# A recurrence, a gated softmax and a ReLU layer on one core: the hand-over into the last stage in a new order

## The chip, the cores and the metric

The kernel runs on one core of a Trainium2 chip. The engines work side by side, each through its own list of instructions in order, and wait for each other by semaphores: PE (TensorE, matrix products), DVE (VectorE), ACT (ScalarE), POOL (GpSimd) and SP (here only a queue of DMA transfers). The metric is the device time of one execution in microseconds.

## The reference

Three layers follow each other. The first is a recurrence over 768 time steps for 4 batches and 8 heads of width 48; the second a layer with a softmax that multiplies its own input and a normalisation; the third a leaky ReLU layer.

```python
def _attn_ref(r, k, v, w, u):
    ...
    for t in range(S):
        cur = np.einsum('bhd,bhe->bhde', u[None] * kt, vt)
        y[:, :, t] = np.einsum('bhd,bhde->bhe', rt, state + cur)
        state = wt[:, :, :, None] * state + np.einsum('bhd,bhe->bhde', kt, vt)

def _moe_ref(x, w_in, w_out, g_ln):          # x: 3072 x 384, d_ff 1024
    h = x @ w_in
    e = np.exp(h - np.max(h, axis=-1, keepdims=True))
    solu = h * e / (np.sum(e, axis=-1, keepdims=True) + 1e-09)
    mu = np.mean(solu, axis=-1, keepdims=True)
    var = np.mean((solu - mu) ** 2, axis=-1, keepdims=True)
    return ((solu - mu) / np.sqrt(var + 1e-06) * g_ln) @ w_out

def _moe2_ref(x, w_in, w_out):               # d_ff 2048
    h = x @ w_in
    return np.maximum(0.01 * h, h) @ w_out
```

## The kernel before

The weights are 64-bit numbers. Their bits are decoded on the chip into 32-bit ones (`decode_exp`, `decode_val`: L58 and L66 to L72 on DVE, L60 on ACT), and each is split into a rounded part and a rest (`hi`, `lo`). A product of two split matrices takes three passes (`passes`).

**Units.** The 3072 tokens are cut into 24 units of 128 (0 to 23), which go through one loop, each in several turns of it: `prep*` and `att_*` make the recurrence of a unit by blocks of time, `x_t` turns the result, `mm1` multiplies by the first layer's input weights into the PSUM tile PH (18 matmuls), `soft_max`, `soft_z`, `soft_c` and `soft_q` make maximum, exponential, product, centring and sum of squares, `z_t` turns the result through PZ, and `z_hi`, `z_lo` split it. A unit's softmax thus runs a turn after its recurrence. Three units make a group of 384 tokens (0 to 7); `mm2(g, m, part)` multiplies a third m of the output for group g, in two halves of 12 matmuls, into the PSUM tile PO or PK, which `mm2_out` copies (L544 on ACT) and writes to memory (`o1_dram`).

**Last stage.** `load_x2`, `split_x2` fetch and split blocks of 512 tokens of that (0 to 7, 768 KB each). Its unit of work is a step (g, c): block g, column chunk c of 16. `mm3` is 9 matmuls into one of two PSUM tiles `h`; ACT and DVE make the leaky ReLU `t` (L701, L702), ACT rounds it (`gh`, L703), `gw_sub` makes the rest `gw`; two steps later `mm4` adds 9 matmuls to the block's output `acc`. The first 32 steps alternate between blocks 0 and 1, c by c. A finished output is scaled on DVE into one of two buffers `ot` and written out. The last layer's weights are decoded in 32 pieces (16 `w2i`, 16 `w2o`) by `dec_step`, some pieces in the hand-over, and one in each of the first steps of the last stage: `load_w2` fetches a piece, `dec_a` starts it, `dec_b` finishes it, `split_hi` and the function that it returns split it.

**Order.** The code runs under a manual schedule: each engine's order is that of the code. The hand-over is what lies between the last unit's `x_t` and the first `mm3`.

Of the kernel before, what the change touches and what calls it, by code (L numbers as in the profile page):

```python
# [19 lines left out]
TOK = B * S  # L20
# [219 lines left out]
def body(tc, trw, nat, w1p, u_p, r, k, v, w, u, w1i, w1o, gln, w2i, w2o, out):  # L240
# [6 lines left out]
    with ExitStack() as ctx:  # L247
# [116 lines left out]
        def prep_bonus(i):  # L364
            a = nats[i]
            pool.tensor_tensor(out=a[:, 1], in0=a[:, 1], in1=a[:, 2], op=ALU.mult)
            pool.tensor_tensor(out=a[:, 1], in0=a[:, 1], in1=ub, op=ALU.mult)

        def prep_diag(i):
            dg = ap2.tile([128, H, 1], F32, name="dg")  # L370
            dve.tensor_reduce(out=dg, in_=nats[i][:, 1], axis=AX.X, op=ALU.add)
            dgs[i] = dg

        def prep_vd(i):
            d = ap2.tile([128, H, D], F32, name="vd")
            vds[i] = d
            pool.tensor_tensor(out=d, in0=nats[i][:, 0], in1=dgs.pop(i).to_broadcast([128, H, D]), op=ALU.mult)
# [24 lines left out]
        def att_u(i):  # L402
            ks, a = kT.pop(i), nats[i]
            for q in range(4):
                for x in range(2):
                    m = 48 if x else 64
                    for c in range(2):
                        pe.matmul(out=PA[64 * x:64 * x + m, c, 256 + 48 * q:304 + 48 * q],  # L408
                                  lhsT=ks[64 * c:64 * c + 64, 112 * q + 64 * x:112 * q + 64 * x + m],
                                  rhs=a[64 * c:64 * c + 64, 0, 4 * x + q], start=True, stop=True)  # L410
# [13 lines left out]
        def att_next(i):  # L424
# [10 lines left out]
        def att_y(i):  # L435
            lt, s, a = L.pop(i), ss[i % 2], nats.pop(i)
# [10 lines left out]
            for q in range(4):  # L447
                for x, (p, e) in enumerate(rows):
                    h = 4 * x + q
                    hs = slice(48 * h, 48 * h + 48)  # L450
                    for c, y in enumerate((y0, y1)):
                        pe.matmul(out=y[64 * c:64 * c + 64, hs], lhsT=s[64 * c:64 * c + 64, x, q],  # L452
                                  rhs=a[64 * c:64 * c + 64, 0, h], start=(h == 0), stop=False, skip_group_check=True)
# [117 lines left out]
        def w1_a():  # L571
# [6 lines left out]
            else:  # L578
                t = mb.tile([128, 512], I32, name="dt")[:, 0:q.shape[1]]
# [41 lines left out]
        pools = [we]  # L621
        w2o_at = []

        def load_w2():
# [3 lines left out]
            t = pools[-1].tile([128, DM, 2], I32, name="w2s", bufs=2 if len(pools) == 1 else 4)  # L628
# [8 lines left out]
        def dec_a():  # L637
# [3 lines left out]
            t = pools[-1].tile([128, DM], I32, name="w2t", bufs=2 if len(pools) == 1 else 4)  # L641
# [3 lines left out]
        def dec_b():  # L645
# [4 lines left out]
            if len(pools) > 1:  # L650
                load_w2()
# [10 lines left out]
        def split_hi():  # L662
            if not ws or (ws[0][0] == "o" and not w2o_at):
                return None
# [6 lines left out]
            else:  # L671
                hi, lo = w2o_at[0][:, c], w2o_at[1][:, c]
# [3 lines left out]
        def load_x2(g):  # L676
            t = xp.tile([128, KC, 512], F32, name="x2")
# [315 lines left out]
```

## Time and profile before

| | |
|---|---|
| median of 3 runs | 823.58 us (823.12 to 824.87) |
| the profiled execution | 822.63 us, span 820.9 us |
| busy: PE, DVE, ACT, POOL | 755.3 (92%), 552.2 (67%), 355.0 (43%), 185.3 (23%) us |
| unit loop up to unit 23's `x_t` | up to about 364 us of the span |
| hand-over | 364 to 406 us |
| last stage | 406 to 813 us, then the last outputs |

The span is the time from the first instruction to the last in the profiler's record; the execution's own time is a little longer. Shares of busy time are means over stages in which different engines set the pace.

### The profile page before, as it was taken

Reading aid. Unit: us, or ns where it says so; the run is one execution under the profiler, and the core shown is the slowest. Engines: PE = TensorE matmul, PEld = TensorE weight load, DVE = VectorE, ACT = ScalarE, POOL = GpSimd, SP = SyncE. Lnnn points to the kernel's source line nnn. Section 1 sums busy time; section 2 is a strip of 40 time slices with the busy share of each in tenths; the row PEclk is TensorE's granted clock in tenths of the full one; section 3 lists DMA queues with packets and bytes.
Section 4 is the critical chain, followed back from the end, with each engine's and each line's share of the span. In section 5 each row is a group of like instructions: output and inputs, shape, how many; then the busy total and the mean of one; then the engine's idle time right before and its main releaser. Section 6 shows DMA issues by size and latency. Waiting matters only on the chain.

```text
span 820.9 us, 14859 instructions
## 1 busy us (share of the span) xinstructions
PE 755.3 (92%) x6197; PEld 623.6 (76%) x6197; DVE 552.2 (67%) x853; ACT 355.0 (43%) x648; POOL 185.3 (23%) x194
## 2 busy tenths in 40 slices
PE   2677889999999999997788999999999999999996
PEld 1344678888888888887666887888888888888884
DVE  6899898888888888868799997243334334334332
ACT  3445455554645555545444554222322322322221
POOL 2211263544545453500211231000100100100000
PEclk9985999999999999999899999999999999999999
DMA  9710334333333445023633430012002001001001
GB/s 297 270 53 15 122 86 125 108 112 108 112 111 109 125 130 149 13 62 106 229 113 92 164 113 0 1 39 77 1 1 77 1 1 39 0 1 40 0 1 42
DMA packets 27805, 66.60 MB, mean 81 GB/s; under 512 B 3804, under 2 KB 13172, under 8 KB 27604
## 3 DMA queue, kind: packets, MB, share of 16 engines
q1 hardware_dynamic: 27300, 64.02, 24.9%
q10 hardware_dynamic: 432, 1.57, 0.6%
q8 instruction: 50, 0.82, 0.4%
q14 instruction: 23, 0.19, 0.1%
HBM read 56.13 MB, written 9.45 MB: 80 GB/s over the span
## 4 chain that ended last, share of the span: by engine, by line
PE 74%; DVE 17%; DMA 3%; issue 2%; ACT 2%; SPq 0%; POOL 0%; DVEq 0%; ACTq 0%
PE acc L716 20%; PE h L695 19%; PE PH L490 11%; PE PO L539 11%; PE PZ L516 3%; DVE w2s L70 3%; PE PA L452 2%; DMA tr<-in_trw_dram 2%; PE PA L408 2%; DVE w2s L68 2%; PE PA L388 2%; DVE w2t L66 2%; DVE t L702 1%; PE PA L461 1%; DVE w2t L72 1%
## 5 line engine op out<-in xcount | busy, mean ns | idle before, releaser
L702 DVE TENSOR_TENSOR t<-t,h 128x512 f32<-128x512 f32 x96 | 65.8, 686 | 133.9 <-ACT t L701 133.9
L701 ACT ACTIVATE t<-h 128x512 f32<-128x512 f32 x96 | 57.3, 597 | 152.4 <-PE h L695 152.4
L695 PE MATMUL h<-x2h,w2ih 128*128 128x512 f32 x288 | 112.2, 390 | 4.4 <-DVE t L702 4.4
L716 PE MATMUL acc<-gw,w2oh 128*128 128x512 f32 x288 | 113.5, 394 | 1.0 <-DVE gw L708 0.8
L716 PE MATMUL acc<-gh,w2ol 128*128 128x512 f32 x288 | 114.0, 396 | 0.0
L695 PE MATMUL h<-x2h,w2il 128*128 128x512 f32 x288 | 113.9, 395 | 0.0
L695 PE MATMUL h<-x2l,w2ih 128*128 128x512 f32 x288 | 113.6, 395 | 0.0
L716 PE MATMUL acc<-gh,w2oh 128*128 128x512 f32 x288 | 112.6, 391 | 0.0
L703 ACT CAST gh<-t 128x512 fp32r<-128x512 f32 x96 | 59.9, 624 | 104.8 <-DVE t L702 104.8
L708 DVE TENSOR_TENSOR gw<-t,gh 128x512 fp32r<-128x512 f32 x83 | 59.3, 714 | 48.9 <-ACT gh L703 46.2
L695 PEld LDWEIGHTS h<-x2h,w2ih 128*128 128x128 f32 x288 | 54.1, 188 | 17.5 <-DVE t L702 5.3
L716 PEld LDWEIGHTS acc<-gw,w2oh 128*128 128x128 f32 x288 | 54.1, 188 | 15.2 <-DVE gw L708 2.5
L695 PEld LDWEIGHTS h<-x2l,w2ih 128*128 128x128 f32 x288 | 54.0, 188 | 13.4
L716 PEld LDWEIGHTS acc<-gh,w2oh 128*128 128x128 f32 x288 | 54.1, 188 | 12.5
L716 PEld LDWEIGHTS acc<-gh,w2ol 128*128 128x128 f32 x288 | 54.1, 188 | 11.6
L695 PEld LDWEIGHTS h<-x2h,w2il 128*128 128x128 f32 x288 | 54.0, 188 | 11.5
L539 PE MATMUL PO<-zh,w1oh 128*128 128x384 f32 x168 | 61.3, 365 | 0.0
L496 ACT ACTIVATE ebuf<-PH,nmax 128x1024 f32<-128x1024 f32 x24 | 26.8, 1117 | 76.3 <-DVE nmax L495 76.3
L490 PE MATMUL PH<-w1ih,xh 128*128 128x512 f32 x144 | 59.1, 411 | 0.6 <-ACT xh L478 0.6
L490 PE MATMUL PH<-w1ih,xl 128*128 128x512 f32 x144 | 57.1, 396 | 0.0
L539 PE MATMUL PO<-zl,w1oh 128*128 128x384 f32 x168 | 57.0, 339 | 0.0
L490 PE MATMUL PH<-w1il,xh 128*128 128x512 f32 x144 | 57.0, 395 | 0.0
(155 smaller groups left out, 1497.3 us busy)
## 6 DMA issues: line engine op xcount, KB each, us to landing
tr<-in_trw_dram SPq DMA_DIRECT2D x23, 675.9 KB, 4.7
nat<-in_nat_dram SPq DMA_DIRECT2D x24, 576.0 KB, 4.1
w2s<-in_moe_w_in_dram SPq DMA_DIRECT2D x48, 128.0 KB, 2.7
w2s<-in_moe_w_out_dram SPq DMA_DIRECT2D x16, 384.0 KB, 3.1
o_dram<-o SPq DMA_DIRECT2D x24, 192.0 KB, 1.9
x<-o_dram SPq DMA_DIRECT2D x6, 768.0 KB, 5.6
out_dram<-ot SPq DMA_DIRECT2D x18, 256.0 KB, 2.1
zh<-in_w1p_dram ACTq DMA_DIRECT2D x3, 512.0 KB, 7.7
```

Source lines behind the costliest of these rows:

```text
L66: dve.scalar_tensor_tensor(out=t, in0=hw, scalar=-2147483648, in1=t, op0=ALU.bitwise_and, op1=ALU.bitwise_or)
L70: dve.scalar_tensor_tensor(out=f(lw), in0=lw.bitcast(U32), scalar=2.0 ** -32, in1=hw, op0=ALU.mult, op1=ALU.add)
L490: pe.matmul(out=PH[:, half], lhsT=a[:, kc], rhs=c[:, kc, 512 * half:512 * half + 512], start=(n == 0), stop=(n == 8))
L496: act.activation(out=ebuf, in_=flat(PH), func=AF.Exp, bias=nmax[:, i:i + 1], accum_out=s_all[:, i:i + 1])
L516: pe.transpose(PZ[c // 4][:, 128 * (c % 4):128 * (c % 4) + 128], zbuf[:, 128 * c:128 * c + 128], ident)
L539: pe.matmul(out=o2[m], lhsT=a[:, c, 128 * m:128 * m + 128], rhs=d[:, c], start=(c == 0 and q == 0), stop=(c == K1 - 1 and q == 2))
L695: pe.matmul(out=h2, lhsT=a[:, kc, 128 * o:128 * o + 128], rhs=d[:, kc], start=(q == 0), stop=(q == 8))
L701: act.activation(out=t, in_=h2, func=AF.Copy, scale=0.01)
L702: dve.tensor_tensor(out=t, in0=t, in1=h2, op=ALU.max)
L703: act.copy(out=gh, in_=t)
L708: (pool if g == 1 and c < 13 else dve).tensor_tensor(out=gw, in0=t, in1=f(gh), op=ALU.subtract)
L716: pe.matmul(out=acc[g][o], lhsT=a[:, c, 128 * o:128 * o + 128], rhs=d, start=(c == 0 and q == 0), stop=(c == K2 - 1 and q == 2))
```

## The change

**The hand-over** is taken out of the loop and written as a list. Unit 23's maximum follows its product, with one decoding step ahead of it in place of two; the products of group 6 stand between unit 23's `mm1` and its `z_t`.

**The last stage's inputs** are loaded straight into the tile of the rest and split in place (`x2_hi`, `x2_lo`), in three pairs of tiles with homes of their own (`xhl2`). Block 0 is loaded before unit 23's product. The first weights (`w2o` chunks 0 to 7) and the first two steps' tiles have homes that are free before the last stage begins.

**The weights**: four pieces are loaded in the unit loop rather than two, the list `wl` alternates `w2i` and `w2o` three chunks apart, two decoding steps stand in the turn of unit 22, five in the hand-over and one in each step of the last stage but steps 3, 7 and 11. `gw_sub` is always on DVE. **The end**: three buffers `ot`, and the last two chunks' products by output thirds 0, 1 and then 2. **The unit's inputs**: v is loaded apart from r and k, whose tile has two buffers in place of three.

```diff
         def load_nat(i, eng):
-            t = ap2.tile([128, 3, H, D], F32, name="nat", bufs=3)
-            nats[i] = t
-            eng.dma_start(out=t, in_=nat[i])
+            t = ap2.tile([128, H, D], F32, name="natv", bufs=3)
+            q = ap2.tile([128, 2, H, D], F32, name="natq")
+            nats[i] = (t, q)
+            eng.dma_start(out=q, in_=nat[i, :, 1:3])
+            eng.dma_start(out=t, in_=nat[i, :, 0])
...
-        wl = [("i", c) for c in range(9)] + [("o", 0), ("o", 1)]
-        for c in range(2, K2):
-            wl += ([("i", c + 7)] if c + 7 < K2 else []) + [("o", c)]
+        wl = [("i", c) for c in range(3)]
+        for c in range(K2):
+            wl += [("o", c)] + [("i", c + 3)] * (c + 3 < K2)
...
         def dec_step():
-            lo = split_hi()
+            ready = len(wa) > 0
             if len(wa) + len(ws) < 3:
                 dec_a()
-            dec_b()
+            lo = split_hi()
+            if ready:
+                dec_b()
             if lo:
                 lo()
...
+            x2[g] = xhl2[g % 3]
+            sp.dma_start(out=f(x2[g][1]), in_=o1_dram[:, :, 512 * g:512 * g + 512])
+
+        def x2_hi(g):
+            xh, xl = x2[g]
+            act.copy(out=xh, in_=f(xl))
+
+        def x2_lo(g, eng):
+            xh, xl = x2[g]
+            eng.tensor_tensor(out=xl, in0=f(xl), in1=f(xh), op=ALU.subtract)
...
-            (pool if g == 1 and c < 13 else dve).tensor_tensor(out=gw, in0=t, in1=f(gh), op=ALU.subtract)
+            dve.tensor_tensor(out=gw, in0=t, in1=f(gh), op=ALU.subtract)
...
-                    ot = lp.tile([128, 512], F32, name="ot", bufs=2)
+                    ot = lp.tile([128, 512], F32, name="ot", bufs=3)
...
-                if i in (18, 19):
+                if 15 <= i < 19:
                     load_w2()
...
+            xhl2.append([rp.tile([128, KC, 512], F32R, name=f"x2{y}0") for y in "hl"])
+            load_x2(0)
+            i = NU - 1
+            x_hi(i)
+            x_lo(i)
+            soft_c(i - 1)
+            soft_q(i - 1)
+            dec_step()
+            mm1(i, 0)
+            mm1(i, 1)
+            soft_max(i)
+            z_t(i - 1)
+            soft_z(i)
+            z_hi(i - 1, 0)
+            z_hi(i - 1, 1)
+            mm2(6, 1, 0)
+            mm2(6, 1, 1)
+            soft_c(i)
+            z_lo(i - 1, 0)
+            z_lo(i - 1, 1)
+            mm2_out(6, 1)
+            dec_step()
+            mm2(6, 2, 0)
+            z_t(i)
+            z_hi(i, 0)
+            z_hi(i, 1)
+            mm2(6, 2, 1)
+            z_lo(i, 0)
+            z_lo(i, 1)
+            soft_q(i)
+            dve.tensor_reduce(out=anyf, in_=flags, axis=AX.X, op=ALU.max)
+            pe.matmul(out=PA[0:1, 0, 0:1], lhsT=anyf, rhs=ones, start=True, stop=True)
+            mm2_out(6, 2)
+            x2_hi(0)
+            es_mb.close()
+            xp = es2.enter_context(tc.tile_pool(name="xp", bufs=1, side="right", reuse_waits="tile"))
+            for cg in range(2):
+                w2o_at.append([xp.tile([128, 4, DM], F32R, name=f"w2o{y}{cg}") for y in "hl"])
+            xhl2.append([xp.tile([128, KC, 512], F32R, name=f"x2{y}1") for y in "hl"])
+            load_x2(1)
+            mm2(7, 0, 0)
+            dec_step()
+            dve.tensor_scalar(out=flag, in0=PA[0:1, 0, 0:1], scalar1=0.0, scalar2=None, op0=ALU.is_gt)
+            x2_lo(0, dve)
+            mm2(7, 0, 1)
+            mm2_out(7, 0)
+            x2_hi(1)
+            mm2(7, 1, 0)
+            dec_step()
+            mm2(7, 1, 1)
+            x2_lo(1, dve)
+            mm2_out(7, 1)
+            mm2(7, 2, 0)
+            dec_step()
+            dve.memset(csc, -0.5)
+            inv_std(nc, csc, s_all, q_all, csc)
+            mm2(7, 2, 1)
+            mm2_out(7, 2)
             es_p.close()
...
+                mm3(g, c)
+                if n % 4 != 3 or n > 12:
                     dec_step()
-                    gw_sub(g, c)
...
+                if n == 8:
+                    scales()
+                if n == 4:
+                    load_x2(2)
+                if c == 0 and 2 <= g and g + 1 < N2:
+                    load_x2(g + 1)
+                if (c == 8 and 2 <= g or c == 14 and g == 1) and g + 1 < N2:
+                    x2_hi(g + 1)
+                    x2_lo(g + 1, pool)
+                if 2 <= n < len(order) - 1:
                     mm4(*order[n - 2])
+            g = N2 - 1
+            mm4(g, K2 - 3)
+            for c, os in ((2, (0, 1)), (1, (0, 1)), (2, (2,)), (1, (2,))):
+                mm4(g, K2 - c, os)
```

On DVE, after unit 23's input has been split (`xl`, the row L482, L484 in the changed kernel), the kernel before has, from the rest of the first decoded piece on (L58 to L72 decode a piece, L674 or L677 is its rest):

```order
L674 TENSOR_TENSOR w2il_109<-w2t,w2ih_108 128x3x128
L58 TENSOR_SCALAR w2t<-w2s 128x384
L66 SCALAR_TENSOR_TENSOR w2t<-w2s,w2t 128x384
L68 TENSOR_SCALAR w2s<-w2s 128x384
L70 SCALAR_TENSOR_TENSOR w2s<-w2s 128x384
L72 SCALAR_TENSOR_TENSOR w2t<-w2s,w2t 128x384
L674 TENSOR_TENSOR w2il_109<-w2t,w2ih_108 128x3x128
L529 TENSOR_TENSOR zl<-PZ_97,zh 128x4x128
L529 TENSOR_TENSOR zl<-PZ_98,zh 128x4x128
L495 TENSOR_REDUCE nmax<-PH 128x1
L500 SCALAR_TENSOR_TENSOR zbuf,z_all<-PH,ebuf 128x1024
```

In the changed kernel this stands there from `xl` on:

```order
L58 TENSOR_SCALAR w2t<-w2s 128x384
L66 SCALAR_TENSOR_TENSOR w2t<-w2s,w2t 128x384
L68 TENSOR_SCALAR w2s<-w2s 128x384
L70 SCALAR_TENSOR_TENSOR w2s<-w2s 128x384
L72 SCALAR_TENSOR_TENSOR w2t<-w2s,w2t 128x384
L677 TENSOR_TENSOR w2il_109<-w2t,w2ih_108 128x3x128
L497 TENSOR_REDUCE nmax<-PH 128x1
L502 SCALAR_TENSOR_TENSOR zbuf,z_all<-PH,ebuf 128x1024
L531 TENSOR_TENSOR zl<-PZ_97,zh 128x4x128
L531 TENSOR_TENSOR zl<-PZ_98,zh 128x4x128
L58 TENSOR_SCALAR w2t<-w2s 128x384
```

One decoding step instead of two, and none of unit 22's rests `zl`, now stand ahead of the maximum `nmax`.

On ACT, from the rounding `zh` of unit 23 on (L509 squares, L544 copies a product out of PSUM, L684 rounds an input block of the last stage), before:

```order
L509 ACTIVATE ebuf,q_all<-zbuf 128x1024
L544 COPY o_4441<-PO 128x384
L673 CAST w2ih_4269<-w2t 128x3x128
L60 ACTIVATE w2t<-w2t,ebias 128x384
L684 CAST x2h<-x_4450 128x1536
L673 CAST w2ih_4269<-w2t 128x3x128
L60 ACTIVATE w2t<-w2t,ebias 128x384
L684 CAST x2h<-x_4452 128x1536
L544 COPY o_4518<-PK 128x384
L673 CAST w2ih_4269<-w2t 128x3x128
```

and in the changed kernel:

```order
L511 ACTIVATE ebuf,q_all<-zbuf 128x1024
L546 COPY o_4467<-PO 128x384
L685 CAST x2h_4333<-x2l_4334 128x1536
L60 ACTIVATE w2t<-w2t,ebias 128x384
L676 CAST w2ih_108<-w2t 128x3x128
L546 COPY o_4519<-PK 128x384
L685 CAST x2h_4479<-x2l_4480 128x1536
L60 ACTIVATE w2t<-w2t,ebias 128x384
```

The second block's rounding has moved behind the copy of PK; both had stood ahead of it.

On DVE in the last stage, from the ReLU `t` of a step of block 1 to the next ReLU, before (POOL had that block's `gw`):

```order
L702 TENSOR_TENSOR t<-t,h_4663 128x512
L58 TENSOR_SCALAR w2t<-w2s 128x384
L66 SCALAR_TENSOR_TENSOR w2t<-w2s,w2t 128x384
L68 TENSOR_SCALAR w2s<-w2s 128x384
L70 SCALAR_TENSOR_TENSOR w2s<-w2s 128x384
L72 SCALAR_TENSOR_TENSOR w2t<-w2s,w2t 128x384
L674 TENSOR_TENSOR w2ol<-w2t,w2oh 128x384
L702 TENSOR_TENSOR t<-t,h_4693 128x512
```

and in the changed kernel:

```order
L706 TENSOR_TENSOR t<-t,h_4645 128x512
L58 TENSOR_SCALAR w2t<-w2s 128x384
L66 SCALAR_TENSOR_TENSOR w2t<-w2s,w2t 128x384
L68 TENSOR_SCALAR w2s<-w2s 128x384
L70 SCALAR_TENSOR_TENSOR w2s<-w2s 128x384
L72 SCALAR_TENSOR_TENSOR w2t<-w2s,w2t 128x384
L677 TENSOR_TENSOR w2il_4328<-w2t,w2ih_4327 128x3x128
L712 TENSOR_TENSOR gw<-t,gh 128x512
L706 TENSOR_TENSOR t<-t,h_4684 128x512
```

The rest `gw` of block 1 has come to DVE, behind the decoding.

## Rows read from the trace of the kernel before

**Rows 1.** Page, part 2: granted TensorE clock in 40 slices of 20.5 us, tenths.
```profile
PEclk9985999999999999999899999999999999999999
```

**Rows 2.** Chain that ended last, middle of the last stage (start us, us, what).
```profile
528.39 2.08 PE acc L716 x9
```

**Rows 3.** Waits of PE, 406 us to the end (total us, times, longest).
```profile
PE h L695 <- DVE t L702: 4.4, 2, 2.4
PE acc L716 <- DVE gw L708: 0.8, 1, 0.8
PE h L726 <- DVE t L702: 0.7, 1, 0.7
```

**Rows 4.** Timeline of PE across the handover (start us, us, engine, line, operation).
```profile
364.59 0.50 PE L490 MATMUL PH<-w1ih,xh 128*128 128x512 f32 x1 [0.62 <-ACT xh L478]
...
368.93 1.04 PE L516 MATMUL PZ<-ident,zbuf 128*128 128x128 f32 x8
...
381.19 1.93 PE L516 MATMUL PZ<-ident,zbuf 128*128 128x128 f32 x8 [4.61 <-ACT zbuf L506]
...
385.81 0.34 PE L539 MATMUL PK<-zh,w1oh 128*128 128x384 f32 x1
...
389.98 0.34 PE L539 MATMUL PO<-zh,w1oh 128*128 128x384 f32 x1
...
398.97 0.69 PE L539 MATMUL PK<-zh,w1oh 128*128 128x384 f32 x1 [4.67 <-ACT o L544]
...
406.09 0.40 PE L695 MATMUL h<-x2h,w2ih 128*128 128x512 f32 x1
```

**Rows 5.** Timeline of DVE after unit 23's first product.
```profile
368.54 0.36 DVE L58 TENSOR_SCALAR w2t<-w2s 128x384 int32<-128x384 int32 x1 [3.41 <-DMA w2s<-in_moe_w_in_dram]
...
375.32 1.22 DVE L495 TENSOR_REDUCE nmax<-PH 128x1 f32<-128x1024 f32 x1
```

**Rows 6.** Timeline of ACT in the handover.
```profile
379.99 1.15 ACT L506 ACTIVATE zbuf<-zbuf,nm_all 128x1024 f32<-128x1024 f32 x1 [1.78 <-POOL nm_all L502]
...
392.99 1.48 ACT L684 CAST x2h<-x 128x1536 fp32r<-128x1536 f32 x1 [5.56 <-DMA x<-o_dram]
```

**Rows 7.** Page, part 6: DMA issues (count, KB each, median us to landing).
```profile
nat<-in_nat_dram SPq DMA_DIRECT2D x24, 576.0 KB, 4.1
...
x<-o_dram SPq DMA_DIRECT2D x6, 768.0 KB, 5.6
```

**Rows 8.** Timeline of DVE over two steps of the last stage.
```profile
429.01 0.68 DVE L702 TENSOR_TENSOR t<-t,h 128x512 f32<-128x512 f32 x1
...
432.39 0.69 DVE L708 TENSOR_TENSOR gw<-t,gh 128x512 fp32r<-128x512 f32 x1
...
433.00 0.68 DVE L702 TENSOR_TENSOR t<-t,h 128x512 f32<-128x512 f32 x1
...
434.45 1.48 DVE L68 TENSOR_SCALAR w2s<-w2s 128x384 int32<-128x384 int32 x1
...
437.51 0.68 DVE L702 TENSOR_TENSOR t<-t,h 128x512 f32<-128x512 f32 x1
```

**Rows 9.** Timeline of POOL in the same two steps.
```profile
434.42 1.29 POOL L708 TENSOR_TENSOR gw<-t,gh 128x512 fp32r<-128x512 f32 x1 [7.20 <-ACT gh L703]
```

**Rows 10.** Timeline of the end: the last product on PE, the last output on DVE.
```profile
812.87 0.39 PE L716 MATMUL acc<-gh,w2ol 128*128 128x512 f32 x1
...
814.81 0.69 DVE L721 TENSOR_TENSOR ot<-acc,cb 128x512 f32<-128x512 f32 x1 [1.50 <-DMA out_dram<-ot]
```

**Rows 11.** Timelines of POOL and DVE in the unit loop.
```profile
331.26 1.47 POOL L366 TENSOR_TENSOR nat<-nat 128x384 f32<-128x384 f32 x1
...
344.47 1.47 POOL L366 TENSOR_TENSOR nat<-nat 128x384 f32<-128x384 f32 x1
...
350.50 0.55 DVE L371 TENSOR_REDUCE dg<-nat 128x8 f32<-128x384 f32 x1
```

**Rows 12.** Timeline of DVE at the start of the program.
```profile
19.82 1.24 DVE L323 TENSOR_TENSOR_SCAN suf<-tr,sel 112x520 f32<-112x520 f32 x1 [0.26 <-DMA tr<-in_trw_dram]
```

More of the change, by code (lines that the diff above doesn't have):

```diff
@@ L627, in load_w2 @@
             s, c = wl.pop(0)
-            t = pools[-1].tile([128, DM, 2], I32, name="w2s", bufs=2 if len(pools) == 1 else 4)
+            t = we.tile([128, DM, 2], I32, name="w2s", bufs=4)
             if s == "i":
@@ L662, in split_hi @@
         def split_hi():
-            if not ws or (ws[0][0] == "o" and not w2o_at):
+            if not ws or (ws[0][0] == "o" and ws[0][1] >= 4 * len(w2o_at)):
                 return None
@@ L671, in split_hi @@
             else:
-                hi, lo = w2o_at[0][:, c], w2o_at[1][:, c]
+                hi, lo = [x[:, c % 4] for x in w2o_at[c // 4]]
             act.copy(out=hi, in_=t)
@@ L860, in body @@
                         load_tr(n + 3, sp)
-                if mo and i < NU - 1:
+                else:
+                    dec_step()
+                if mo:
                     mm1(i, 0)
@@ L877, in body @@
                 w1_step(i)
-                if att:
-                    att_x(n)
-                if has2 and i < NU:
-                    if i == NU - 1:
-                        mm2(g, m, 0)
+                att_x(n)
+                if has2:
                     mm2(g, m, 1)
                     mm2_out(g, m)
-                if att:
-                    x_t(n)
+                x_t(n)
                 if mo:
                     soft_z(i)
-                if i == NU - 1:
-                    pe.matmul(out=PA[0:1, 0, 0:1], lhsT=anyf, rhs=ones, start=True, stop=True)
-                    dve.tensor_scalar(out=flag, in0=PA[0:1, 0, 0:1], scalar1=0.0, scalar2=None, op0=ALU.is_gt)
@@ L905, in body @@
-                if i > NU:
-                    dec_step()
-            es_ma.close()
+            es_a.close()
+            rp = es2.enter_context(tc.tile_pool(name="rp", bufs=1, side="right", reuse_waits="tile"))
+            for cg in range(1, 4):
+                w2i_h.append(rp.tile([128, KC, 512], F32R, name=f"w2ih{cg}"))
+                w2i_l.append(rp.tile([128, KC, 512], F32R, name=f"w2il{cg}"))
+            xhl2.append([rp.tile([128, KC, 512], F32R, name=f"x2{y}0") for y in "hl"])
+            load_x2(0)
@@ L911, in body @@
             ps_o = es2.enter_context(tc.tile_pool(name="ps_o", bufs=2, space=PSUM, reuse_waits="tile"))
[L912 to L915 removed]
             order = [(g, c) for c in range(K2) for g in range(2)]
             order += [(g, c) for g in range(2, N2) for c in range(K2)]
[L918 to L930 removed]
+            for n in range(len(order)):
+                if n == 2:
+                    es_ma.close()
+                    lp = es2.enter_context(tc.tile_pool(name="lp", bufs=1, reuse_waits="tile"))
+                    for cg in range(2, 4):
+                        w2o_at.append([lp.tile([128, 4, DM], F32R, name=f"w2o{y}{cg}") for y in "hl"])
+                    xhl2.append([lp.tile([128, KC, 512], F32R, name=f"x2{y}2") for y in "hl"])
+                    cb = lp.tile([128, TOK], F32, name="cb")
+                    lp_at.append(lp)
+                g, c = order[n]
+                mm3(g, c)
+                if n % 4 != 3 or n > 12:
+                    dec_step()
+                gw_sub(g, c)
+                if n == 8:
[8 more added lines that the diff above has]
+                if 2 <= n < len(order) - 1:
```

160 lines of the change are left out of this document (46 added, 114 removed).

## The prediction

> **What bounds the kernel now.** I went from the end backwards. In the chain that ended last, the middle of the last stage is nothing but PE: 9 matmuls take 2.08 us and the next 9 follow at once [rows 2], so a step of 18 takes 4.16 us and the 96 steps at least 399.4 us. The stage starts at 406.09 [rows 4], and its last matmul starts at 812.87 [rows 10] and is passed some 0.23 later (2.08 by 9): 407.0 us. So 7.6 us of the stage are not PE's work. The view of PE's waits names 5.9 of them: 4.4 and 0.7 for the ReLU on DVE, 0.8 for a rest `gw` on DVE [rows 3].
>
> PE's timeline then shows the hand-over. Its first matmul stands at 364.59. At 381.19 PE has waited 4.61 us for unit 23's centred product, at 398.97 another 4.67 us for ACT to free a PSUM tile [rows 4]. The granted clock falls there: the slice from 390 to 410 us has an 8 in a long row of nines [rows 1], so that part of it ran at the lower of the two levels (1.2 and 2.4 GHz). Its price stands in PE's timeline. At full clock 24 products take 4.17 us (385.81 to 389.98); after the second wait the same 24 take 7.12 (398.97 to 406.09), 2.95 more. After the first wait 8 transposes and 12 products take 4.62 us (381.19 to 385.81), against 1.04 for such transposes at 368.93 and half of 4.17: 1.5 more [rows 4].
>
> **Why PE waits.** The first wait is DVE's order. Unit 23's product is done at 368.93, when the next work on PE starts [rows 4], but the maximum starts on DVE at 375.32 [rows 5]. Up to 368.54 DVE waits 3.41 us for a piece of weights, and two pieces and unit 22's rests stand in its list ahead of the maximum [rows 5]. The second wait is ACT's order: it stands 5.56 us at the rounding of an input block whose transfer has not landed, up to 392.99 [rows 6], and the copy that frees PE's tile is behind that.
>
> **The hand-over after the change.** PE's instructions are the same ones, so I take away what its timeline shows as waiting and as lower clock. Will the waits be gone?
> *Unit 23's softmax.* From the start of the maximum (375.32) to the start of the transposes (381.19) the chain takes 5.87 us [rows 4, 5], with POOL's step in it, for which ACT waited 1.78 [rows 6]. One decoding step is still ahead of the maximum. Such a step is 2.7 us: a whole round of DVE in the last stage takes 3.99 (429.01 to 433.00), of which `gw` is 0.61 (432.39 to 433.00) and the ReLU 0.68 [rows 8]. It lies beside the product (364.59 to 368.93, 4.34 us), and its piece is one of four loaded units earlier, so the 3.41 us wait for a piece has no ground. The maximum then starts at about 369.1 and the transposes can start at 375.0. Meanwhile PE has unit 22's transposes and 36 products of group 6, 1.0 plus 6.3 us, up to about 376.2. The wait is covered with about 1 us to spare; without that cover each us of delay would cost one, and after some us the clock too.
> *The input blocks.* Block 0 is asked for during unit 23's product, some 10 us before ACT rounds it, and a transfer takes 5.6 us [rows 7]. Block 1 is asked for behind the output of (6, 2), whose last product ends at 379.3 (376.2, transposes, 12 products) and is copied by 380; so it lands at 386 and is rounded (1.48, as in [rows 6]) at 387.5. Behind that rounding on ACT stand one decoding step's two instructions and the copy out of (7, 1); the copy that frees PK for (7, 2) is ahead of it. DVE must then end the decoding step, of whose 2.7 us under 2 can still be open, and make block 1's rest (taken like the rounding), by about 391; PE reads it with the stage's second `mm3`, at about 394.5. That is 3 us to spare.
> So both waits (4.61 + 4.67) and both stretches at the lower clock (1.5 + 2.95) go: **13.7 us**, and the last stage starts at 392.4. The 0.62 us before unit 23's product stays. The bounds are 0 (both waits come back elsewhere) and 14.3.
>
> **The last stage.** While weights are decoded, DVE sets the pace: two steps take 8.50 us there (429.01 to 437.51) and 8.32 on PE. The step of block 0 takes 3.99, that of block 1 takes 4.51, although POOL makes its `gw` [rows 8]. Without `gw` it should take 3.38, so 1.13 are lost in it. The row shows where: an L68 of 1.48 us, which ends when POOL's subtraction does (434.42 plus 1.29) or just behind [rows 8, 9]. With `gw` on DVE both steps take 3.99, 7.98 for two, under PE's 8.32. The 13 subtractions cost DVE 13 x 0.61 = 7.9 us and spare it 13 x 1.13 = 14.7.
> The Trainium skill, "SBUF — State Buffer", section "SBUF: two separate sides", says that DVE and GpSimd share a pair of ports under an exclusive lock, held for the whole instruction. The trace agrees (1.48 beside 1.29). The rule speaks against what POOL keeps, block 2's rest with three times the columns: by an estimate of 3 x 1.29 = 3.9 us it would hold DVE once, and the sum would be 806.0 if PE felt all of it. I set it at nothing: it stands at step 29, the last with decoding, and from there DVE has 4.16 less 0.68 and 0.61, 2.9 us a step, without work.
> More decoding falls into the stage than before: 6 of 32 pieces are finished when it starts, 11 before, since the hand-over is shorter. The chunk c of `w2o` is split in step 2c+1 from c = 6 on and read in the next one's `mm4`. From the end of `mm3` it takes ACT's part of the ReLU (taken like DVE's, with 0.2 to start, 0.9), DVE's 0.68 and 2.7, 4.3 in all; PE reads the rest of the chunk 4.16 plus two matmuls later, 4.6. That is tight, 0.3 us, but holds. Three steps without decoding (3, 7, 11) let DVE catch up ahead of the transposes of step 8, where PE waits now (L726). I take the 5.9 listed and 1.0 of the 1.7 unlisted as gone, and 0.6 as new waits in the first steps, where DVE still ends the hand-over's last piece: **6.3 us**. Bounds: 0 (DVE still paces) and 7.6.
>
> **The end.** The last output waits 1.50 us on DVE for the transfer that frees one of two buffers [rows 10]. A third buffer removes it: the last product is over by 813.3, when DVE can start. **1.5 us**; bounds 1.0 and 1.6. The new order of the last products only makes the first two outputs earlier.
>
> **Costed at nothing.** The split of v from r and k: as many bytes, 24 more transfers on SP. The load for unit n+2 now waits for the sum `dg` of unit n (two buffers), and all later transfers on SP are behind it. `dg` runs at 350.50; POOL multiplies the next unit's r and k about 7 us after `dg` (344.47 against 350.50 less 13.21) and that of unit n+2 one period later, 331.26 to 344.47 being 13.21 [rows 11]. So 20.4 us lie between, and the transfer takes 4.1 [rows 7]. At the start of the program DVE is nearly always busy and waited only 0.26 us for unit 1's inputs at 19.82 [rows 12]; the transfers ahead of them are the same bytes, so I give it 0, and 1 us either way to the range. Decoding in unit 22 and the split in place are the same instructions as before.
>
> **Sum.** 13.7 + 6.3 + 1.5 = 21.5 us off the profiled 822.63: 801.1. The median of the runs is 0.95 above that execution: 802.1.
>
> **The rivals.**
> *A, the sum:* 802.1, its own range 799.5 to 804.5.
> *B, DVE goes on pacing the first third of the last stage.* For it: DVE's 7.98 is only 4% under PE's 8.32, the margin for `w2o` is 0.3 us, and five more pieces must be decoded there. Against it: the long L68 is explained by POOL. It gives back 6.3: 808.4.
> *C, the hand-over closes in part.* The margin of 1 us for the transposes, or the 3 us for block 1, is used up by a late POOL step or transfer. A wait of 2 us with 1.5 for the clock gives 805.6.
> *D, the waits come back whole elsewhere in the hand-over,* so that the list does not do what it says: 802.1 + 13.7 = 815.8. Against it: nothing ahead of the chains is left that waits.
> *E, slower.* The split loads hold SP, and each unit's inputs come late. From unit 2 to 23 each unit must last 1.0 us longer (21.5 by 22) to eat the gain; at 1.2 us the time is 828.5. It decides when the transfer needs more than 16 us longer than the 4.1 that it takes, for which nothing speaks.
> The Trainium skill, "DMA: Bandwidth & Descriptors", section "Anatomy of one DMA — SWDGE (gpsimd) path", gives every transfer a fixed 2.0 us. By that rule an estimate for 24 more transfers with none hidden is 48 us; the trace's 20.4 us of lead say that all of it is hidden.
>
> **How the numbers follow.** A 0.62, B 0.15, C 0.15, D 0.05, E 0.03. The range is 799 to 808.5: below, all upper bounds (14.3 + 7.6 + 1.6 = 23.5, so 800.1) and 1 us from the start; above, B. It leaves out D, E and a part of B, some 0.15. A change of 0.2% (1.6 us) is about what a measurement of this kernel can tell from none. Faster 0.96, the same 0.01, slower 0.03.
>
> **What would show it.** PE at unit 23's product still near 364.6, which settles the start, E and the split loads. No wait at unit 23's transposes near 376, none at a product into PK, and the granted clock at one through the hand-over; the first `mm3` near 392.4. In the last stage waits of PE under 1.5 us in total, no L68 of 1.48, two DVE steps in 8.32 with idle time in them. The third `ot` without a wait for a transfer. I would be wrong if PE's waits moved to the first `mm3` of block 1 (a late block 1), to `acc` behind a rest of `w2o` (B), or if units lasted longer than 13.21.

## The result

| | before | changed |
|---|---|---|
| median of the runs | 823.46 us (4 runs) | 802.91 us (4 runs, 799.17 to 803.66) |
| ratio of the medians, 95% interval | | 0.9738 [0.9706, 0.9771] |
| the profiled execution | 822.63 us, span 820.9 us | 803.08 us, span 801.0 us |

The forecast of 802.1 us was right in size; its last term was not right in cause, and its middle term hid a cost that I had not seen. That the sum comes so close is in part luck: its errors have both signs, and the start of the hand-over alone scatters by more (below). The difference of the two spans is 19.9 us. PE's timeline divides it: unit 23's product starts 0.9 us later, from there to the first `mm3` 14.26 us are gone, from there to the end of the last product 4.96, and behind it 1.6.

**The hand-over.** The timeline of PE in the changed kernel (start us, us, engine, line, operation, then the wait):
```profile
365.49 0.50 PE L492 MATMUL PH<-w1ih,xh 128*128 128x512 f32 x1 [0.62 <-ACT xh L480]
...
376.97 1.03 PE L518 MATMUL PZ<-ident,zbuf 128*128 128x128 f32 x8
...
388.57 0.34 PE L541 MATMUL PK<-zh,w1oh 128*128 128x384 f32 x1
...
392.73 0.40 PE L698 MATMUL h<-x2h,w2ih 128*128 128x512 f32 x1
```
Against [rows 4] the bracket at unit 23's transposes and the one at the product into PK are gone; the 0.62 ahead of the product stays. From 365.49 to 392.73 are 27.24 us, where it was 41.50. The table of busy time by stretch shows the clock with it (stretch, its us, PE busy, granted clock, DMA share, GB/s), first before, then changed:
```profile
364.60:406.10 41.50, 32.22 (x157) 0.88 0.54 174
```
```profile
365.50:392.70 27.20, 27.20 (x156) 1.00 0.47 153
```
PE worked 32.22 us in the one and 27.20 in the other on the same products, so 9.3 us were the waits', and most of the other 5.0 the lower clock's. The timeline of DVE shows why the first wait went:
```profile
370.05 1.22 DVE L497 TENSOR_REDUCE nmax<-PH 128x1 f32<-128x1024 f32 x1 [0.88 <-PE PH L492]
```
The maximum [rows 5] now waits for the product itself, not for a piece of weights. And the timeline of ACT, for both:
```profile
374.14 1.16 ACT L508 ACTIVATE zbuf<-zbuf,nm_all 128x1024 f32<-128x1024 f32 x1 [0.61 <-POOL nm_all L504]
...
384.61 0.48 ACT L546 COPY o<-PK 128x384 f32<-128x384 f32 x1 [1.70 <-PE PK L541]
...
387.64 1.48 ACT L685 CAST x2h<-x2l 128x1536 fp32r<-128x1536 f32 x1 [2.55 <-DMA x2l<-o_dram]
```
The centred product is ready at 375.30, 1.7 us before PE's transposes. ACT still waits for an input block, as in [rows 6], but the copy that frees PK stands ahead of that wait and is done at 385.1, long before PE comes to PK at 388.57.

**The last stage.** The waits of PE over 360 to 801 us (total us, times, longest), which answer to [rows 3], are all of them these two:
```profile
PE PH L492 <- ACT xh L480: 0.6, 1, 0.6
PE acc L722 <- DVE gw L712: 0.5, 1, 0.5
```
Two steps on DVE, as in [rows 8]:
```profile
425.49 0.69 DVE L706 TENSOR_TENSOR t<-t,h 128x512 f32<-128x512 f32 x1 [1.86 <-ACT t L705]
...
429.78 0.69 DVE L706 TENSOR_TENSOR t<-t,h 128x512 f32<-128x512 f32 x1 [0.21 <-ACT t L705]
...
431.24 0.36 DVE L68 TENSOR_SCALAR w2s<-w2s 128x384 int32<-128x384 int32 x1
...
433.98 0.69 DVE L706 TENSOR_TENSOR t<-t,h 128x512 f32<-128x512 f32 x1
```
No L68 of 1.48 us is left, and no other decoding instruction of DVE in the stage that takes over 0.6. But the chain that ended last shows what I had not expected (start us, us, what). In chunks 0 to 7:
```profile
435.42 2.08 PE h L698 x9
437.50 2.11 PE acc L722 x9
```
in chunks 8 to 15:
```profile
493.90 2.07 PE h L698 x9
495.97 2.09 PE acc L722 x9
```
and in block 2:
```profile
546.10 2.10 PE acc L722 x9
548.20 2.10 PE h L698 x9
```
Nine matmuls took 2.08 in both products before [rows 2]. Now `mm4` takes 2.11 to 2.12 with chunks 0 to 7 of `w2o`, and both products take 2.10 in blocks 2 and 5, whose input lies in the third pair of `x2` tiles (from chunk 8 on, `mm4` takes 2.09 there). Nothing waits in these places: the matmuls themselves follow at 232 to 235 ns instead of 231. On PE's timeline steps 10 to 89 (counted from 0, as in the prediction) take together 1.7 us more than 4.16 each; the stage's 402.05 us are 1.35 above the forecast.

**The end.** The last product on PE, then the outputs on DVE, which answer to [rows 10]:
```profile
794.55 0.39 PE L722 MATMUL acc<-gh,w2ol 128*128 128x512 f32 x1
```
```profile
792.94 1.37 DVE L726 TENSOR_TENSOR ot<-acc,cb 128x512 f32<-128x512 f32 x2 [1.37 <-PE acc L722]
794.98 0.69 DVE L726 TENSOR_TENSOR ot<-acc,cb 128x512 f32<-128x512 f32 x1 [0.67 <-PE acc L722]
```

### The profile page after: what moved, and what is told of

It reads as the page before. It is cut to its first block, busy times and chain, and to the rows that moved or that the text cites. A ratio compares the mean times of both kernels' runs of the same rounds, so it can differ in the third digit from the quotient of the medians.

```text
span 801.0 us, 14910 instructions
## 1 busy us (share of the span) xinstructions
PE 751.9 (94%) x6197; PEld 620.8 (77%) x6197; DVE 547.5 (68%) x866; ACT 354.9 (44%) x648; POOL 167.0 (21%) x181
## 4 chain that ended last, share of the span: by engine, by line
PE 87%; DVE 6%; DMA 2%; ACT 2%; issue 1%; POOL 0%; SPq 0%; DVEq 0%; ACTq 0%; POOLq 0%
PE acc L722 25%; PE h L698 24%; PE PH L492 11%; PE PO L541 11%; PE PZ L518 3%; PE PA L454 2%; DMA tr<-in_trw_dram 2%; PE PA L410 2%; PE PA L390 2%; PE PA L463 1%; PE PO L608 1%; PE PK L386 1%; PE PZ L475 1%; PE PA L444 1%; PE PK L541 1%
## 5 line engine op out<-in xcount | busy, mean ns | idle before, releaser
L712 DVE TENSOR_TENSOR gw<-t,gh 128x512 fp32r<-128x512 f32 x96 | 69.1, 719 | 47.4 <-ACT gh L707 44.6
L689 POOL TENSOR_TENSOR x2l<-x2l,x2h 128x1536 fp32r<-128x1536 f32 x4 | 14.1, 3515 | 285.4 <-ACT x2h L685 285.4
```

Source lines behind the costliest of these rows:

```text
L712: dve.tensor_tensor(out=gw, in0=t, in1=f(gh), op=ALU.subtract)
```

## The experiments

In each, "hand-over" is the time on PE's timeline from the first matmul of unit 23's product to the first `mm3` (27.24 us in the changed kernel), and "stage" that from there to 0.23 us behind the start of the last matmul (402.05). They come from one profiled execution of each kernel; the start of unit 23's product, which no experiment touches, lies anywhere from 361.87 to 367.36 us in them, so whole times carry a scatter of some us. With the changed order these lengths don't: where no edit bears on it, the hand-over is 27.23 to 27.25 each time. With the old order it is 41.50, 40.35 and 40.15 in three executions (before, 2, 7), as its two waits come out at 4.0 to 4.7.

| kernel | median us | ratio to before, 95% interval | hand-over | stage |
|---|---|---|---|---|
| changed | 802.91 | 0.9738 [0.9706, 0.9771] | 27.24 | 402.05 |
| 1: 32 bytes, last stage | 800.17 | 0.9704 [0.9681, 0.9727] | 27.24 | 399.07 |
| 2: before, `w2o` moved by 32 bytes | 826.56 | 1.0030 [1.0011, 1.0049] | 40.35 | 411.88 |
| 3: `gw` on POOL | 806.18 | 0.9781 [0.9757, 0.9805] | 27.23 | 407.94 |
| 4: late maximum | 804.59 | 0.9756 [0.9729, 0.9783] | 28.79 | 401.99 |
| 5: two `ot` | 802.46 | 0.9740 [0.9706, 0.9775] | 27.25 | 402.78 |
| 6: 416 bytes, last stage | 794.01 | 0.9635 [0.9608, 0.9661] | 27.23 | 392.95 |
| 7: before, 416 bytes | 818.15 | 0.9932 [0.9908, 0.9956] | 40.15 | 403.54 |
| 8: block 1 first on ACT | 804.15 | 0.9768 [0.9732, 0.9805] | 28.12 | 402.03 |
| 9: no steps without decoding | 805.05 | 0.9767 [0.9727, 0.9807] | 27.25 | 403.65 |
| 10: 160 bytes | 793.45 | 0.9618 [0.9577, 0.9659] | 27.24 | 393.50 |
| 11: 928 bytes | 792.75 | 0.9626 [0.9586, 0.9666] | 27.23 | 392.97 |
| 12: 416 bytes, `t`, `gh`, `gw`, `ot` alone | 798.86 | 0.9704 [0.9671, 0.9737] | 27.23 | 399.28 |

### Undoing the parts of the change

**Experiment 4: the maximum late again.**
```
 dec_step()
 mm1(i, 0)
 mm1(i, 1)
-soft_max(i)
+dec_step()
 z_t(i - 1)
-soft_z(i)
 z_hi(i - 1, 0)
 z_hi(i - 1, 1)
+z_lo(i - 1, 0)
+z_lo(i - 1, 1)
+soft_max(i)
+soft_z(i)
 mm2(6, 1, 0)
 mm2(6, 1, 1)
 soft_c(i)
-z_lo(i - 1, 0)
-z_lo(i - 1, 1)
 mm2_out(6, 1)
-dec_step()
```


> The changed kernel with VectorE's second decoding step and unit 22's two rests back ahead of unit 23's maximum, so that the maximum stands again behind two pieces and the rests; PE's order is the same. My theory: the maximum starts about 5 us later (375 instead of 370.05), zbuf comes that much later than the 1.7 us of spare that the chain has, and PE waits 3 to 4 us at unit 23's transposes, with up to 1.5 more for the lower clock: 3 to 5.5 us longer from unit 23's product to the first mm3 than 27.24. Rival (the wait was for the piece of weights that came late, 3.41 us on VectorE, not for the order): the piece is here in time, and the hand-over is at most 1 us longer.

The timelines of DVE and of PE:
```profile
375.07 1.22 DVE L497 TENSOR_REDUCE nmax<-PH 128x1 f32<-128x1024 f32 x1
```
```profile
380.30 0.87 PE L518 MATMUL PZ<-ident,zbuf 128*128 128x128 f32 x6 [1.28 <-ACT zbuf L508]
```
The product starts at 367.36 here, so the maximum comes 7.71 us behind it, where the changed kernel has 4.56 and the one before 10.73 (375.32 less 364.59). Its order alone makes 3.15 of the 6.17 us between those two; 1.7 of them are spare, and PE waits 1.28. The hand-over is 1.55 us longer, less than either of my two figures for the theory. The rest of before's wait was the piece that came late (3.41 us in [rows 5]), which here is in time. So both readings hold in part: the order makes the chain late, and the late piece made most of the 4.61. The second half of this is a difference of two kernels; no run delays the piece alone.

**Experiment 8: block 1 ahead of the copy on ACT.**
```
-mm2_out(7, 0)
 x2_hi(1)
+mm2_out(7, 0)
```


> The changed kernel with the rounding of input block 1 ahead of the copy of (7, 0) on ACT. My theory (what stands behind the block's transfer on ACT decides when PE's tile is freed): the rounding starts at 387.64 in the changed kernel's time and takes 1.48, the copy 0.48, so PE, which comes to the tile at 388.57, waits for it 1.0 to 1.3 us, and the hand-over is that much longer than 27.24. Rival (in the kernel before PE did not wait for the copy but for something else): no wait at the product into PK.

PE at the product into PK:
```profile
388.91 0.44 PE L541 MATMUL PK<-zh,w1oh 128*128 128x384 f32 x1 [0.60 <-ACT o L546]
```
and ACT ahead of it:
```profile
387.01 1.48 ACT L685 CAST x2h<-x2l 128x1536 fp32r<-128x1536 f32 x1 [4.53 <-DMA x2l<-o_dram]
388.39 0.47 ACT L546 COPY o<-PK 128x384 f32<-128x384 f32 x1
```
The wait of before is back in small, with the same releaser, and the hand-over is 0.88 us longer, a little less than I had expected. ACT waits for the transfer in the changed kernel too, but nothing that PE needs stands behind it there. The place in ACT's list costs 0.60 of the 4.67, and not all of it.

**Experiment 3: `gw` of block 1 on POOL.**
```
-dve.tensor_tensor(out=gw, in0=t, in1=f(gh), op=ALU.subtract)
+(pool if g == 1 and c < 13 else dve).tensor_tensor(out=gw, in0=t, in1=f(gh), op=ALU.subtract)
```


> The changed kernel with gw of block 1 back on POOL for its first 13 chunks. My theory (POOL's subtraction holds VectorE's next instruction, 1.13 us of each pair of steps): VectorE's L68 of 1.48 us is back in the steps of block 1, a pair takes 8.5 instead of 8.36, and the last stage is 2 to 5 us longer than 402.05. Rival (the pace of VectorE came from elsewhere, the decoding order or the steps without decoding): no more than 0.5 us, with an L68 of 1.48 or without.

POOL, and DVE in the same step:
```profile
430.58 1.50 POOL L712 TENSOR_TENSOR gw<-t,gh 128x512 fp32r<-128x512 f32 x1 [6.19 <-ACT gh L707]
```
```profile
430.96 1.54 DVE L70 SCALAR_TENSOR_TENSOR w2s<-w2s 128x384 f32<-128x384 uint32 x1
```
and PE's waits over the whole stretch behind 360 us name who comes late:
```profile
PE acc L722 <- DVE w2ol L677: 3.7, 7, 0.6
```
The stage is 5.9 us longer, more than I expected. The instruction that is held is mostly L70, which takes 0.56 elsewhere in this run: eight of them take 1.53 to 1.54, and two L68 1.47 to 1.48. In the last stage of the kernel before it was seven L70 and three L68, so the L68 of [rows 8] was one case of several. The Trainium skill, "SBUF — State Buffer", section "SBUF: two separate sides", describes a port pair that GpSimd and VectorE hold in turn, for a whole instruction. The trace agrees: 1.54 us beside POOL's 1.50, and in the changed kernel four `gw` of 1.29 to 1.68 us on DVE instead of 0.69, each beside one of POOL's four rests of an input block, 3.51 us. They stand where DVE has time, and no wait of PE follows them.

**Experiment 9: decoding in every step.**
```
-if n % 4 != 3 or n > 12:
-    dec_step()
+dec_step()
```


> The changed kernel with a decoding step in every step of the last stage, also in steps 3, 7 and 11, where it has none. My theory (the three steps let VectorE catch up ahead of the transposes of step 8, where PE waited in the kernel before): PE waits again there, 0.5 to 1 us. Rival: VectorE has enough time in any case, and PE's waits stay at the 0.5 us of the first mm4.

PE's waits:
```profile
PE h L698 <- DVE t L706: 1.3, 1, 1.3
```
The wait is back, at the first `mm3` behind the transposes (429.02), a little longer than I had expected, and the stage is 1.6 us longer: the three steps are what lets DVE catch up there. In the kernel before, 2.0 of the 4.4 us of [rows 3] stand at this `mm3`.

**Experiment 5: two `ot` buffers.**
```
-ot = lp.tile([128, 512], F32, name="ot", bufs=3)
+ot = lp.tile([128, 512], F32, name="ot", bufs=2)
```


> The changed kernel with two ot buffers instead of three. My theory: the third output needs the buffer of the first, whose transfer starts near 793.7 and takes 3.1 us; VectorE waits for it until about 796.7 instead of starting at 794.98, and the end comes 1.5 to 1.8 us later. Rival (the new order of the last products alone gives the transfer its time): less than 0.5 us.

DVE's last row:
```profile
794.10 0.69 DVE L726 TENSOR_TENSOR ot<-acc,cb 128x512 f32<-128x512 f32 x1 [1.89 <-PEq L960]
```
The last matmul starts at 792.45 here, so the third output starts 1.65 us behind it, 1.22 more than in the changed kernel. Yet from that matmul to the end of the span it is 6.63 us, against 6.49 in the changed kernel and 5.86 to 7.05 in the ten kernels with three buffers. The three kernels with the old order have 7.97 to 8.04. So what the end gained is there without the third buffer; a gain from it does not show above the scatter of 1.2 us. My theory's 1.5 to 1.8 fell. The rival's number held, but not its reason, since DVE still waits. The transfer of the last output shows where the gain of the buffer went (KB, us from issue to landing), before, in the changed kernel and here:
```profile
out_dram<-ot SPq DMA_DIRECT2D x1, 256.0 KB, 3.1
```
```profile
out_dram<-ot SPq DMA_DIRECT2D x1, 256.0 KB, 3.8
```
```profile
out_dram<-ot SPq DMA_DIRECT2D x1, 256.0 KB, 2.7
```
Issued 1.2 us earlier, closer behind the other two outputs, it takes 1.1 us longer.

### The nine matmuls that take 2.04 to 2.12 us

The tiles of the last stage lie in two parts of SBUF. No trace shows addresses; where the tiles start was worked out from the order and the sizes of the pools: on the upper side all start 480 bytes behind a multiple of 512; the tiles of the pool `lp` start 64 behind one. Before, `w2o`, `gh` and `gw` lay in `lp`, the `x2` and `w2i` tiles on the upper side, so that the two operands of a matmul agreed. In the changed kernel chunks 0 to 7 of `w2o` are on the upper side, and the third `x2` pair is in `lp`: they meet operands from the other side in just the places that are slow. An empty tile at the head of a pool moves what is behind it:
```
 lp = es2.enter_context(tc.tile_pool(name="lp", bufs=1, reuse_waits="tile"))
+lp.tile([128, 8], F32, name="pad")
```
**Experiment 1** has these 32 bytes, **6** has 104 elements (416 bytes), **10** has 40 (160 bytes), **11** has 232 (928 bytes).

> The changed kernel with an empty tile of 32 bytes put first into the pool of the last stage, so that chunks 8 to 15 of w2o, the third pair of x2 tiles, cb, gh, gw, t and ot start 32 bytes further on; in the changed kernel these start at multiples of 64 bytes, all other operands of the last stage 32 bytes behind one. Theory 'remainder': 9 matmuls take 2.10 to 2.12 us instead of 2.08 where the stationary and the moving operand have different remainders by 64. Then all are alike here: 2.08 for every 9, the last stage 1.5 to 2.2 us shorter than the changed kernel's 402.05, and the time about 801. Rival 'side': what counts is that one operand lies in the upper and one in the lower part of the memory, whatever the remainder. Then 2.10 to 2.12 stay where they are, and the stage lasts 402. Rival 'traffic': the extra time is that of other engines' accesses. Then nothing changes either, and the slow groups end with the decoding.

The chain of experiment 1, in chunks 8 to 15 and in block 2:
```profile
495.53 2.05 PE acc L722 x9
...
545.19 2.10 PE acc L722 x9
547.29 2.09 PE h L698 x9
```
The stage is 3.0 us shorter, so "side" and "traffic" are out. But "remainder by 64" does not fit either: all starts agree by 64 (and by 128) here, block 2 keeps 2.09 to 2.10, and other groups went under the 2.08 that I had taken for PE's pace.

**Experiment 2** moved `w2o` away from `gh` and `gw` in the kernel before:
```
+lp.tile([128, 8], F32, name="pad", bufs=1)
 w2oh = lp.tile([128, K2, DM], F32R, name="w2oh", bufs=1)
 w2ol = lp.tile([128, K2, DM], F32R, name="w2ol", bufs=1)
 w2o_at += [w2oh, w2ol]
+lp.tile([128, 8], F32, name="pad2", bufs=1)
 cb = lp.tile([128, TOK], F32, name="cb", bufs=1)
```


> The kernel before with an empty tile of 32 bytes ahead of w2oh and another behind w2ol: w2o is moved by 32 bytes, gh and gw keep their remainder by 64; nothing else changes. Theory 'remainder': mm4 now has operands with different remainders in all 96 steps, and its 9 matmuls take 2.11 instead of 2.08: 2.2 to 2.9 us more in the last stage (some of the first steps wait for VectorE anyhow), about +2.5 us on the time. Rivals 'side' and 'traffic': no change, within 0.5 us.

```profile
493.23 2.10 PE acc L716 x9
495.33 2.09 PE h L695 x9
```
Eight steps take 33.49 instead of 33.28 us once the first ten are over, and from there to the end the stage is 2.0 us longer, by nothing but addresses; `mm3`, whose tiles stayed where they were, is slower too (2.09). The rest of the stage's 4.9 us lies in its first ten steps, where DVE is waited for (47.63 against 44.77 us); experiment 7 has 47.67 there, so I don't put that down to the edit. In both, PE comes to the stage with a hand-over that is 1.2 to 1.3 us shorter, and its first wait for DVE is 3.7 us in place of 2.4.

> The changed kernel with an empty tile of 416 bytes first in the pool of the last stage: all operands of mm3 and mm4, gh, gw, t and ot then start 480 bytes behind a multiple of 512 (in the changed kernel chunks 8 to 15 of w2o, the third x2 pair, gh, gw, t and ot stand at 64). Theory 'remainder by 512': what counts is the distance of the two operands' starts by 512 bytes; 9 matmuls took 2.05 at best where it is 0 and 2.08 to 2.12 where it is 32, 96 or 128. Then nearly all groups take 2.05 to 2.07 here, a step 4.10 to 4.14 instead of 4.16 to 4.20, the last stage lasts 395 to 398 instead of 402.05, the time is about 797. Rival 'remainder by 64 or 128' : this kernel is like the one with 32 bytes, 399.1 for the stage with 2.09 to 2.10 left in chunks 0 to 7 and in blocks 2 and 5. Rival 'side': 2.09 to 2.12 stay in those groups.

> The kernel before with an empty tile of 416 bytes ahead of w2oh, so that w2o, cb, gh, gw, t and ot, too, start 480 bytes behind a multiple of 512. Theory 'remainder by 512': the engines that write t, gh and gw and PE then all work at the same distance, 9 matmuls take 2.05 instead of 2.08 where no engine is waited for, and the last stage is 2 to 4 us shorter than 407.0. Rival (only the distance between the two operands of one matmul counts; it is 0 in the kernel before too): within 0.5 us of 407.0.

Experiment 6, block 2:
```profile
546.58 2.04 PE h L698 x9
548.62 2.04 PE acc L722 x9
```
Experiment 7, in the same block:
```profile
547.44 2.04 PE h L695 x9
549.48 2.04 PE acc L716 x9
```
With one remainder for all tiles of the stage, nine matmuls take 2.04 in every block, a matmul every 227 ns, and the changed kernel's stage takes 392.95: 9.1 us less. The kernel before gains 0.64 in eight steps (32.64 against 33.28) once the first ten are over, 6.4 us from there to the end; its whole stage is only 3.5 us shorter, because of the first ten. Its median is 6.8 us lower than that of the kernel before beside it (824.96). So [rows 2] was not PE's pace, only the pace of that placement. In experiment 7 PE still waits 4.0 and 4.3 us in the hand-over and 5.7 for the ReLU.

> The changed kernel with an empty tile of 160 bytes first in the pool of the last stage: its tiles now agree with those of the upper side by 128 and by 256 bytes (224 and 480 behind a multiple of 512), but not by 512. If 256 is the period that counts: 2.04 for every 9 matmuls, 393 for the stage, as with 416 bytes. If it is 512: as with 32 bytes, about 399, or between, with 2.04 in groups whose two operands agree by 512 and 2.06 to 2.11 in chunks 0 to 7 and blocks 2 and 5.

> The changed kernel with an empty tile of 928 bytes first in the pool of the last stage: its tiles agree with those of the upper side by 512 bytes (480), and not by 1024 (992 and 480). If 512 is enough: 2.04 for every 9 matmuls, and 393 for the stage. If the period is 1024: 2.06 to 2.11 in some groups again, and 395 to 402.

One row of each, experiment 10 and then 11:
```profile
548.06 2.04 PE acc L722 x9
```
```profile
547.63 2.04 PE acc L722 x9
```
Both are like experiment 6 from the eleventh step on. By the starts that were worked out, agreement by 256 bytes is enough (experiment 10); by 128 it is not (experiment 1).

**Experiment 12** moved only `t`, `gh`, `gw` and `ot`, which ACT and DVE write in the steps:
```
 cb = lp.tile([128, TOK], F32, name="cb")
+lp.tile([128, 104], F32, name="pad")
```


> The changed kernel with an empty tile of 416 bytes behind cb instead of ahead of w2o: t, gh, gw and ot, which ACT and VectorE write, start 480 bytes behind a multiple of 512; chunks 8 to 15 of w2o and the third x2 pair stay at 64. Theory 'pair and writers': a matmul is slowed by its two operands' distance by 512 and by the distance of ACT's and VectorE's accesses. Then chunks 0 to 7 of w2o and mm3 outside blocks 2 and 5 take 2.04 to 2.05, chunks 8 to 15 and mm3 of blocks 2 and 5 2.08 to 2.12, and the stage about 397 to 399. Rival 'writers only': 2.04 everywhere, 393. Rival 'pair only': mm3 outside blocks 2 and 5 keeps its 2.07 to 2.08, chunks 0 to 7 take 2.04, chunks 8 to 15 2.10 to 2.12.

The chain in chunks 0 to 7 of block 3, in chunks 8 to 15 of blocks 0 and 1, and in block 2:
```profile
620.02 2.04 PE h L698 x9
622.06 2.04 PE acc L722 x9
```
```profile
492.93 2.10 PE acc L722 x9
495.02 2.08 PE h L698 x9
```
```profile
547.35 2.08 PE acc L722 x9
549.43 2.11 PE h L698 x9
```
"Writers only" and "pair only" are out: there are slow groups though the writers' tiles agree, and `mm3` of blocks 3 and 4 falls from 2.08 to 2.04 in chunks 3 to 10 (in blocks 0 and 1 up to chunk 8) although its own operands didn't move. "Pair and writers" has its times about right (399.28), but it does not say why `mm3` takes 2.08 in chunks 11 to 15, where its own operands agree with each other and with the writers' tiles, and only the `mm4` between them doesn't. That addresses other than those of a matmul's own operands count is shown; which accesses meet is open.

**The best version** is thus the changed kernel with an empty tile ahead of the last stage's own: 792.75 to 794.01 us with 928, 160 or 416 bytes, whose intervals overlap, about 9 to 10 us below the changed kernel's 802.91.

## Why the prediction was right

**Hand-over, 13.7 forecast, 14.26 measured.** Both waits and the lower clock went, as in the working. The maximum came at 370.05, 4.56 behind the start of the product (I had 4.5), the spare time at the transposes was 1.7 us (1.0), the block's rounding started at 387.64 (386). Most of the 0.56 that the forecast missed is in what a wait costs. Its bracket counts from the end of the last matmul, which takes 0.34 us there, while without a wait the next one starts 0.17 us behind that matmul's start. So each of the two waits took 0.17 more than its bracket, and 0.16 more went between the first wait and the product at 385.81, mainly because eight transposes delay the next product by 0.79 and not by the 1.04 that I had taken from their row. The experiments show the same, with the first matmul behind a wait slower as well (0.28 us to the next one in experiment 8, 388.91 to 389.19): a bracket of 1.28 costs 1.55 us (experiment 4), one of 0.60 costs 0.88 (8), seven that sum to 3.7 make most of 5.9 (3). And 14.26 is one execution's figure: against the hand-overs of experiments 2 and 7, which have the old order, 13.1 and 12.9 are gone.

Experiments 4 and 8 bring each wait back, smaller than in the kernel before, since each had a second cause that stayed removed. For the first it is the late piece. For the second it is not the transfer: ACT's wait for it was over at 392.99, 1.3 us before PE began to wait (394.30, the start of the bracket of 4.67), just as in experiment 8 (387.01 and 388.31). What kept PE waiting stood behind it on ACT in the kernel before:
```profile
396.57 0.62 ACT L60 ACTIVATE w2t<-w2t,ebias 128x384 int32<-128x384 int32 x1 [1.69 <-DVE w2t L58]
397.09 1.46 ACT L684 CAST x2h<-x 128x1536 fp32r<-128x1536 f32 x1
398.45 0.47 ACT L544 COPY o<-PK 128x384 f32<-128x384 f32 x1
```
Two blocks' roundings and a decoding step with its wait for DVE lay between, 5.46 us from the first rounding to the copy. In experiment 8 one rounding is ahead of it, 1.38 us, since block 0 was rounded at 380.08. So loading and rounding block 0 early made most of this wait go, and the order the last 0.60; the working named only the transfer and the order. This is read from the rows; no run puts block 0 back, as none delays the piece of weights.

**Last stage, 6.3 forecast, 4.96 measured: the term that was mis-sized.** Its waits went as forecast, and a little better: of 7.6 us beside PE's work some 0.9 are left, where I had set 1.3 (0.6 new and 0.7 unlisted). Of the cause that I gave, POOL's `gw`, experiment 3 shows what it costs in the new order (5.9 us), and experiment 9 what the steps without decoding spare (1.6). They don't cover all of the waits: 3.2 of the 5.9 listed us (2.4 at 412.7, 0.8 at 416.1) stood ahead of POOL's first `gw`, which starts at 417.41. DVE came to the stage's first ReLU only at 412.01 there, 5.9 us behind the first `mm3`, with decoding steps in a row ahead of it; in the changed kernel it comes at 395.64, 2.9 behind. My working did not name this, and no run undoes it alone. What failed is the step ahead of them: "a step of 18 takes 4.16 us and the 96 steps at least 399.4 us". I took the pace of one placement for PE's. The change moved tiles to homes whose starts don't agree, and the same 18 matmuls take 4.16 to 4.21 there, 1.7 us in all; with starts that agree they take 4.08. I had priced the new homes by the transfers and waits that they spare, and given the addresses no thought.

**The end, 1.5 forecast, 1.6 measured: right in size by luck.** I gave it all to the third `ot` buffer. Its last transfer is issued 1.15 us behind the last matmul instead of 2.66, which is the 1.5 that I had. But the transfer then takes 0.7 longer, and with two buffers it lands no later (5.10 us behind that matmul, against 4.32 to 5.52 with three). I also wrote that "the new order of the last products only makes the first two outputs earlier"; with two buffers it makes the third 0.3 us earlier as well. The other 0.7 us lie where I had not looked, behind the landing: from there to the end of the span it was 2.26 to 2.52 us in the three kernels with the old order and is 1.52 to 1.78 in the eleven others. No run shows which part of the change did that.

**The start, 0 forecast.** The 0.9 us by which unit 23's product came later are within what the profiled executions scatter with the same instructions ahead of it: 361.87 to 367.36, on average 364.7 in the eleven kernels with the changed unit loop, 364.9 in the three with the old one. So the split loads cost nothing that can be seen, and E is out. The section of the Trainium skill, "DMA: Bandwidth & Descriptors", that the prediction names for a fixed 2.0 us is about transfers that GpSimd issues; these are issued on SP, and nothing of the 48 us showed.

**The rivals.** B did not come: DVE has time in the steps. The part of the 6.3 that is missing is the matmuls' pace. C and D did not come: no wait moved elsewhere in the hand-over.

## What to carry to other kernels

Where a wait is removed by an order, check each engine's list apart: experiments 4 and 8 show that a wait can have two causes, for with the old order alone 1.28 of 4.61 and 0.60 of 4.67 us came back. What stands behind a late transfer on its engine can cost more than the transfer. A pace read from a stretch in which one engine never waits is the pace of that stretch, not the engine's best: when a change moves tiles, compare the time of equal groups of matmuls before and after, not only the waits. Where fp32 matmuls follow without a gap, an empty tile at the head of a pool that makes the starts agree by 256 bytes is a cheap try; here 416 bytes gave 9.1 us in the last stage, more than the forecast's 6.3.

## What was unexpected in the hardware

The time from one 128x512 matmul to the next was 227 ns in every block where all tiles of the stage start at the same distance from a multiple of 256 bytes, and up to 235 ns where they don't, with no wait shown there and the granted clock at 1.00 in both. In this stage of 1728 matmuls that was 9.1 us between the changed kernel and the same one with 416 empty bytes.
